# A fused attention and feed-forward kernel: 512-token steps in a fixed order, and scores on the four corners of the array

## The chip, the cores and the metric

The kernel runs on one core of a Trainium2 chip. The metric is device time in microseconds of one execution. Before the change the median of three runs is 714.71 us (709.36, 714.71, 715.33). The profile comes from one further execution, which took 712.24 us.

In the profile, PE is the matrix engine and PEld its loading of the stationary operand, DVE the vector engine, ACT the scalar (activation) engine, POOL the GpSimd engine, and SP the engine whose queue issues all DMA transfers here. Matrix products are written to accumulation memory (PSUM), which the kernel uses as eight banks of 128 rows x 512 float32.

## The reference

Attention with a narrow window and block summaries, and a feed-forward layer on its result (float32 throughout; batch 4, 8 heads, 768 tokens, head dimension 64; model width 512, hidden width 2048):

```python
block, window = 32, 16
k_sum = k.reshape(B, H, nb, block, D).max(axis=3)
v_sum = v.reshape(B, H, nb, block, D).mean(axis=3)
scores_l = scale * (q @ k^T), masked to |i - j| < window
scores_s = scale * (q @ k_sum^T) + log(block)
a = softmax(concatenate([scores_l, scores_s], -1))
attn = a @ concatenate([v, v_sum])
x = attn with heads side by side, as (3072 tokens, 512)
h = x @ w_in
out = (h * tanh(softplus(h))) @ w_out
```

The gate h * tanh(softplus(h)) is the activation that the code calls Mish. The feed-forward weights arrive as 64-bit floats and are converted on the chip.

## The kernel before

**Chunks and units.** The 3072 tokens are cut into 12 chunks of 256 (CH); three chunks make a batch element. Attention is done in units: one chunk and one pair of heads (HP = 4 pairs), so 48 units. A unit handles its 256 queries in four blocks of 64 (NQ = 4, QT = 64). Each block sees 96 keys of its window and the 24 block summaries, 120 columns (KA).

**One unit.** `att_load_keys` and `att_load_values` (L200 to L229) have SP fetch the unit's queries, window keys and window values; POOL copies the key summaries beside the window keys, a DMA copies the value summaries. For the first chunk of a batch, `key_summaries` and `value_summaries` (L163, L176) load all keys and values of the head pair into `stage` buffers, and DVE reduces them. `att_scores` (L240) does the scores. From chunk 1 on the two heads of a pair are done in one matmul per block: the host lays the queries out as a block-diagonal 128x128 operand (head 0 in rows and columns 0 to 63, head 1 in 64 to 127, zeros elsewhere), and the 128 rows of the second operand are the keys of both heads. In the first chunk the two heads are separate matmuls, each on its own 64 rows and 64 columns:

```python
nc.tensor.matmul(ps[:, s * KA:(s + 1) * KA], u["qk"][:, s, 0:P], u["qk"][:, s, P:],
                 start=True, stop=True)
```

DVE then adds the mask, scales and takes the row minimum of the negated scores (L261), ACT takes exponentials with their sum (L266), DVE the reciprocal (L269, L270), and POOL multiplies (L271). `att_transpose` (L274) turns the four blocks on PE and ACT copies them out; `att_values` (L283) multiplies with the values, each head into its own 64 columns of the array, over 120 rows. The result is split in a high part (ACT, L296) and a rest (DVE, L297), `xh` and `xl`, so that three matmuls on rounded operands replace one float32 matmul.

**Feed-forward steps.** A step is (c, fp): chunk c, and fp a pair of the 16 blocks of 128 hidden features. `ff_in` (L303) does 2 x 4 x 3 = 24 matmuls of 256 columns into one bank; `ff_act` (L317) applies Mish on ACT and splits into `gh` and `gl`; `ff_out` (L329), two steps later, does 2 x 2 x 3 = 12 matmuls of 512 columns into two output banks that stay in use over the chunk's eight steps. The first two chunks' steps are interleaved, so that each new weight block serves twice (16 steps); chunks 2 to 11 follow one after another (80 steps).

**Weights.** `load_weight` (L107) loads a 128x512 block of 64-bit floats into a `stage` buffer (3 buffers); DVE, ACT and POOL rebuild float32 from the two halves of the bits and split it (L116 to L125). 32 such blocks are done once, in the first part.

**Order.** The program is written step by step (L381 to L399): `ff_in` and `ff_act` of step i, scores or values of the units due, weight loads, `ff_out` of step i - 2, and transposes. This is only a priority: a planner with costs of its own then orders every engine's instructions, and may pull work of later steps forward where operands and buffers are free. The table `at` sets a unit's scores at some step k, its transposes at k + 1 and its values at k + 2. Chunk 2's four units have k = 7, 9, 11, 13; chunk c > 2 has its units during chunk c - 1, one every two steps. Queries, keys and values are requested one unit ahead (L391).

**Banks.** Two banks for `ff_in` (`ps_h`), four for outputs (`ps_o`), two for all attention from chunk 1 on (`ps_a`).

Of the kernel before, what the change touches and what calls it, by code (L numbers as in the profile page):

```python
# [36 lines left out]
NP_ = NFC // 2  # L37
EARLY = 10
NR = (S - CH) // P
LEAD = 4  # L40
AHEAD = 3
# [14 lines left out]
def fused_kernel(ctx: ExitStack, tc: tile.TileContext, q0, qk, kt, v0, vw, vs, w_in, w_out, out):  # L56
# [32 lines left out]
    nc.gpsimd.memset(first[:, 0:WIN], NEG / SCALE)  # L89
    last = const.tile([P, KA], F32, name="last")  # L90
    nc.gpsimd.tensor_copy(last, base)
    nc.gpsimd.memset(last[:, KW - WIN:KW], NEG / SCALE)
# [14 lines left out]
    def load_weight(src, hi, lo, name):  # L107
# [4 lines left out]
        f = ff.tile([P, WP], F32, tag="f", name=f"{name}_f", bufs=3)  # L112
        x = ff.tile([P, WP], U32, tag="x", name=f"{name}_x", bufs=2)
# [48 lines left out]

    def key_summaries(b, hp):  # L163

        if b == 0:
            ks = first_att.tile([P, WIN + S], F32, tag="ks", name=f"ks{b}_{hp}")
            nc.gpsimd.memset(ks[:, 0:WIN], 0.0)
        else:
            ks = stage.tile([P, WIN + S], F32, tag="stage", name=f"ks{b}_{hp}")
        nc.sync.dma_start(ks[:, WIN:], kt[b, hp])  # L170
        km = att.tile([P, NB], F32, tag="km", name=f"km{b}_{hp}", bufs=HP + 2)
        nc.vector.reduce_max(km, ks[:, WIN:].rearrange("p (n j) -> p n j", j=BLK), axis=AX.X)
        summary[b, hp] = [km]
        return ks

    def value_summaries(b, hp):  # L176
# [16 lines left out]
        vsum = stage.tile([VP, BLK, BLK], F32, tag="stage", name=f"vsum{b}_{hp}")  # L193
        nc.sync.dma_start(vsum, vs[b, hp].rearrange("p (d j) -> p d j", j=BLK))
# [40 lines left out]
    def att_psum(c, name):  # L235

        pool, tag = (ps_o, "o") if c == 0 else (ps_a, "a")
        return pool.tile([P, 512], F32, tag=tag, name=name)

    def att_scores(c, hp):  # L240
        u = units[c, hp]
        th = c % CPB
        ps = att_psum(c, f"sc{c}_{hp}")
        for s in range(NQ):
            if c > 0:
                nc.tensor.matmul(ps[:, s * KA:(s + 1) * KA], u["qk"][:, s, 0:P], u["qk"][:, s, P:],  # L246
                                 start=True, stop=True)
                continue
            for h in range(2):
                r = slice(h * D, (h + 1) * D)  # L250
                q = u["q"][r, s * QT:(s + 1) * QT]
                nc.tensor.matmul(ps[r, s * KA:s * KA + KW], q, u["k"][r, s * QT:s * QT + KW],
                                 start=True, stop=True)
                nc.tensor.matmul(ps[r, s * KA + KW:(s + 1) * KA], q, summary[0, hp][0][r, :],
                                 start=True, stop=True)
        pr = (att if c else first_att).tile([P, NQ, KA], F32, tag="pr", name=f"pr{c}_{hp}")

        nm = small.tile([P, NQ], F32, tag="nm", name=f"nm{c}_{hp}")
        for s in range(NQ):
            m = first if th == 0 and s == 0 else last if th == CPB - 1 and s == NQ - 1 else base  # L260
            nc.vector.tensor_tensor_reduce(  # L261
                out=pr[:, s, :], in0=ps[:, s * KA:(s + 1) * KA], in1=m, scale=-SCALE,
                scalar=-NEG, op0=ALU.add, op1=ALU.min, accum_out=nm[:, s:s + 1])
        sm = small.tile([P, NQ], F32, tag="sm", name=f"sm{c}_{hp}")
        for s in range(NQ):
            nc.scalar.activation(pr[:, s, :], pr[:, s, :], AF.Exp, scale=-1.0, bias=nm[:, s:s + 1],  # L266
                                 accum_out=sm[:, s:s + 1])
        rs = small.tile([P, NQ], F32, tag="rs", name=f"rs{c}_{hp}")
        nc.vector.tensor_scalar_add(rs, sm, 1e-9)  # L269
        nc.vector.reciprocal(rs, rs)  # L270
        nc.gpsimd.tensor_mul(pr, pr, rs.unsqueeze(2).broadcast_to([P, NQ, KA]))  # L271
        u["p"] = pr
# [10 lines left out]
    def att_values(c, hp):  # L283
        u = units.pop((c, hp))
        if c not in xs:
            xs[c] = (xp.tile([P, HP, CH], F32R, tag="xh", name=f"xh{c}"),
                     xp.tile([P, HP, CH], F32R, tag="xl", name=f"xl{c}"))
        xh, xl = xs[c]
        ps = att_psum(c, f"x_ps{c}_{hp}")
        for s in range(NQ):  # L290
            for h in range(2):
                d = slice(h * D, (h + 1) * D)
                x = ps[d, s * QT:(s + 1) * QT]
                pt = u["pt"][:, s, h * QT:(h + 1) * QT]
                nc.tensor.matmul(x, u["v"][:, s, d], pt, start=True, stop=True)  # L295
        nc.scalar.copy(xh[:, hp, :], ps[:, :CH])  # L296
        nc.vector.tensor_sub(xl[:, hp, :], ps[:, :CH], xh[:, hp, :].bitcast(F32))  # L297
# [5 lines left out]
    def ff_in(c, fp):  # L303
        i = c, fp
        xh, xl = xs[c]

        pool, tag = (ps_a, "a") if c == NCH - 1 and fp in (NP_ - 1, NP_ - 3) else (ps_h, "h")
        ph = pool.tile([P, 2, CH], F32, tag=tag, name=f"ph{c}_{fp}")
        for j in range(2):
            wh, wl = (weight(0, part, 2 * fp + j) for part in range(2))  # L310
            for cc in range(NCC):
                for n, (w, x) in enumerate(((wh, xh), (wh, xl), (wl, xh))):
                    nc.tensor.matmul(ph[:, j, :], w[:, cc * P:(cc + 1) * P], x[:, cc, :],  # L313
                                     start=(cc == 0 and n == 0), stop=(cc == NCC - 1 and n == 2))
        st[i] = {"h": ph.rearrange("p j t -> p (j t)")}

    def ff_act(c, fp):  # L317

        s = st[c, fp]
        g = ff.tile([P, 2 * CH], F32, tag="g", name=f"g{c}_{fp}", bufs=3)  # L320
        nc.scalar.activation(g, s["h"], AF.Mish)  # L321
        gh = ff.tile([P, 2 * CH], F32R, tag="gh", name=f"gh{c}_{fp}", bufs=3)
        gl = ff.tile([P, 2 * CH], F32R, tag="gl", name=f"gl{c}_{fp}", bufs=3)
# [120 lines left out]
```

## Time and profile before

| | |
|---|---|
| runs, us | 709.36, 714.71, 715.33; median 714.71 |
| profiled execution, us | 712.24 |
| its span, us | 710.5 |
| PE busy | 672.8 us (95%), 4960 matmul records |
| PEld busy | 603.6 us (85%) |
| DVE busy | 301.1 us (42%) |
| ACT busy | 354.2 us (50%) |
| POOL busy | 111.5 us (16%) |
| mean granted PE clock | 0.976 |
| DMA | 70.56 MB, mean 99 GB/s |

The span is the time from the first to the last instruction; the execution's own time has 1.7 us more around it. Busy shares are means over stages: the first quarter of the span, in which the weights are converted, looks different from the rest, so the stages have to be read apart. Matmuls are pipelined, and a matmul's own duration (291 ns for 256 columns) overlaps the next one's; what one costs in a dense row is read from the distance of the starts. A name such as `po<-w_early_out_hi,gh` says which tile is written from which; "x12" is a count. A float32 matmul appears as two records.

### The profile page before, as it was taken

To read this page: it belongs to the slowest core of one execution; us is meant where nothing else is said; L and a number is where in the kernel's file an instruction comes from. 1 tells how busy PE (TensorE), PEld (TensorE's weight loads), DVE (VectorE), ACT (ScalarE), POOL (GpSimd) and SP (SyncE) were. 2 spreads that over 40 slices of the span, in tenths; PEclk is the share of its full clock that TensorE was granted. 3 is DMA by queue.
4 is the path that set the end of the run, shared out by engine and by line. 5 is a ranking of instruction groups with operands and counts; after the bars stand their busy time and mean duration, and the time that the engine had idled before them with its cause. 6 is when DMAs were issued, how large, how long until landed. Compare 5 with 4: busy or idle time off the path is not lost.

```text
span 710.5 us, 12644 instructions
## 1 busy us (share of the span) xinstructions
PE 672.8 (95%) x4960; PEld 603.6 (85%) x4960; DVE 301.1 (42%) x872; ACT 354.2 (50%) x776; POOL 111.5 (16%) x151
## 2 busy tenths in 40 slices
PE   4978788799999999999999999999999999999998
PEld 3767677688898998998998998998998998998996
DVE  4899989952322334443223233222222322322211
ACT  2767755544556644644644644644644644644110
POOL 3454554301010010010100100100100100010000
PEclk9969899899999999999999999999999999999999
DMA  9876655772221323531311311311311311300000
GB/s 276 239 235 204 184 171 155 216 230 88 88 71 44 111 56 104 161 89 43 116 43 43 116 43 44 117 44 43 116 43 43 117 43 44 115 15 1 30 1 30
DMA packets 30683, 70.56 MB, mean 99 GB/s; under 512 B 4768, under 2 KB 9504, under 8 KB 30624
## 3 DMA queue, kind: packets, MB, share of 16 engines
q1 hardware_dynamic: 30624, 69.76, 32.2%
q8 instruction: 39, 0.64, 0.4%
q14 instruction: 20, 0.16, 0.1%
HBM read 61.15 MB, written 6.29 MB: 95 GB/s over the span
## 4 chain that ended last, share of the span: by engine, by line
PE 79%; DVE 11%; DMA 4%; issue 2%; ACT 2%; SPq 0%; POOL 0%; DVEq 0%; POOLq 0%
PE ph L313 34%; PE po L340 33%; PE sc L246 6%; PE x_ps L295 3%; DVE w_x L116 3%; PE pt_ps L278 2%; DVE w_x L117 2%; DVE w_f L122 2%; DMA ks<-kt 1%; DMA vsum<-vs 1%; DMA vw<-vw 1%; DVE w_f L120 1%; ACT pr L266 1%; DVE gl L326 1%; DVE vq L196 1%
## 5 line engine op out<-in xcount | busy, mean ns | idle before, releaser
L313 PE MATMUL ph<-xh,w_early_in_hi 128*128 128x256 f32 x480 | 138.7, 291 | 3.2 <-ACT w_early_in_hi L124 2.4
L313 PE MATMUL ph<-xh,w_early_in_lo 128*128 128x256 f32 x480 | 139.1, 291 | 2.2 <-POOL w_early_in_lo L125 2.2
L313 PE MATMUL ph<-xl,w_early_in_hi 128*128 128x256 f32 x480 | 138.9, 290 | 1.2 <-DVE xl L297 1.2
L325 DVE CAST gh<-g 128x512 fp32r<-128x512 f32 x80 | 34.3, 429 | 209.3 <-ACT g L321 196.6
L271 POOL TENSOR_TENSOR pr<-pr,rs 128x480 f32<-128x480 f32 x48 | 49.0, 1021 | 348.2 <-DVE rs L270 309.7
L313 PEld LDWEIGHTS ph<-xh,w_early_in_hi 128*128 128x128 f32 x480 | 93.9, 196 | 7.1 <-ACT w_early_in_hi L124 3.2
L313 PEld LDWEIGHTS ph<-xl,w_early_in_hi 128*128 128x128 f32 x480 | 93.8, 196 | 3.9 <-DVE xl L297 1.7
L313 PEld LDWEIGHTS ph<-xh,w_early_in_lo 128*128 128x128 f32 x480 | 93.9, 196 | 3.2 <-POOL w_early_in_lo L125 2.6
L340 PE MATMUL po<-w_early_out_hi,gh 128*128 128x512 f32 x240 | 94.3, 396 | 2.5 <-ACT gh L325 2.5
L340 PE MATMUL po<-w_early_out_hi,gl 128*128 128x512 f32 x240 | 95.6, 398 | 0.0
L340 PE MATMUL po<-w_early_out_lo,gh 128*128 128x512 f32 x240 | 95.0, 396 | 0.0
L321 ACT ACTIVATE g<-ph 128x512 f32<-128x512 f32 x96 | 57.4, 598 | 67.0 <-PE ph L313 66.5
L313 PE MATMUL ph<-xh,w_late_in_hi 128*128 128x256 f32 x288 | 82.5, 287 | 0.1
L313 PE MATMUL ph<-xh,w_late_in_lo 128*128 128x256 f32 x288 | 81.9, 284 | 0.1
L313 PE MATMUL ph<-xl,w_late_in_hi 128*128 128x256 f32 x288 | 81.1, 282 | 0.0
L266 ACT ACTIVATE pr<-pr,nm 128x120 f32<-128x120 f32 x192 | 73.7, 385 | 5.8 <-DVE nm L261 5.3
L321 ACT ACT_TABLE_LOAD x44 | 56.5, 1283 | 38.7 <-PE ph L313 38.3
L326 DVE TENSOR_TENSOR gl<-g,gh 128x512 fp32r<-128x512 f32 x96 | 70.7, 736 | 8.1 <-ACT gh L325 5.5
L296 ACT CAST xh<-x_ps 128x256 fp32r<-128x256 f32 x48 | 17.9, 372 | 100.7 <-PE x_ps L295 100.7
L280 ACT COPY pt<-pt_ps 120x512 f32<-120x512 f32 x48 | 28.1, 586 | 71.9 <-PE pt_ps L278 71.5
L266 ACT ACT_TABLE_LOAD x43 | 55.2, 1283 | 8.4 <-DVE nm L261 7.8
L340 PE MATMUL po<-w_late_out_hi,gl 128*128 128x512 f32 x144 | 56.7, 394 | 1.6 <-DVE gl L326 1.6
(75 smaller groups left out, 1149.9 us busy)
## 6 DMA issues: line engine op xcount, KB each, us to landing
qk<-qk SPq DMA_DIRECT2D x44, 496.0 KB
vw<-vw SPq DMA_DIRECT2D x48, 192.0 KB
w<-w_in SPq DMA_DIRECT2D x16, 512.0 KB
w<-w_out SPq DMA_DIRECT2D x16, 512.0 KB
ks<-kt SPq DMA_DIRECT2D x16, 384.0 KB
out<-o SPq DMA_DIRECT2D x24, 256.0 KB
vsum<-vs SPq DMA_DIRECT2D x12, 384.0 KB
vw<-vm SPq DMA_DIRECT2D x44, 48.0 KB
```

The costliest lines, as they stand in the source:

```text
L116: nc.vector.tensor_scalar(out=x, in0=low, scalar1=29, scalar2=None, op0=ALU.logical_shift_right)
L246: nc.tensor.matmul(ps[:, s * KA:(s + 1) * KA], u["qk"][:, s, 0:P], u["qk"][:, s, P:], start=True, stop=True)
L266: nc.scalar.activation(pr[:, s, :], pr[:, s, :], AF.Exp, scale=-1.0, bias=nm[:, s:s + 1], accum_out=sm[:, s:s + 1])
L271: nc.gpsimd.tensor_mul(pr, pr, rs.unsqueeze(2).broadcast_to([P, NQ, KA]))
L280: nc.scalar.copy(pt.rearrange("p s q -> p (s q)"), ps[:KA, :])
L295: nc.tensor.matmul(x, u["v"][:, s, d], pt, start=True, stop=True)
L296: nc.scalar.copy(xh[:, hp, :], ps[:, :CH])
L313: nc.tensor.matmul(ph[:, j, :], w[:, cc * P:(cc + 1) * P], x[:, cc, :], start=(cc == 0 and n == 0), stop=(cc == NCC - 1 and n == 2))
L321: nc.scalar.activation(g, s["h"], AF.Mish)
L325: (nc.scalar.copy if c < 2 else nc.vector.tensor_copy)(gh, g)
L326: nc.vector.tensor_sub(gl, g, gh.bitcast(F32))
L340: nc.tensor.matmul(po[c][t], g[:, tok], w, start=(fc == 0 and n == 0), stop=(fc == NFC - 1 and n == 2))
```

## The change

- **Steps.** From the second pair of chunks on, a step is (g, fc): a pair of chunks (TG = 512 tokens) and one block of 128 hidden features. `ff_in` then has 4 x 3 = 12 matmuls of 512 columns, and `ff_out` 4 x 3 = 12 of 512 into four output banks, one for each 128 tokens. There are again 80 such steps. The first pair keeps its 256-token steps. `xh` and `xl` hold a pair of chunks.
- **Order.** The 80 steps are inside `tc.manual_schedule()`: each engine does its instructions in the order of the program. The first 16 steps are still ordered by the planner. Chunk 2's units have k = 6, 7, 8, 9 and chunk 3's k = 10, 11, 12, 13; later units come one every two steps during the pair of chunks before theirs. In an iteration: `ff_in`, Mish, values (of the unit two steps before), scores, split, normalization, loads, `ff_out` of step i - 2, transposes (of the unit one step before).
- **Scores.** Each block and head is a matmul of its own, on 64 rows (the head) and 64 columns (odd or even block), so that a block pair of both heads uses the four 64x64 corners. The zeros of the block-diagonal layout are no longer read, though still loaded. Each head writes into a bank of its own, so a unit's scores take two banks.
- **Banks and buffers.** `ff_in`, scores, transposes and values share four banks (`ps_w`); four remain for outputs. The weight scratch, the activations and the output copies share six buffers (before: 3 + 2, 3 and 2).
- **Smaller.** Summaries are requested two units ahead (`load_ahead`); the output copies alternate between ACT and DVE; the edge masks hold only for the half of the rows with the first or last block.

The diff, cut:

```diff
+LEAD = 4
+CG = 2
+TG = CG * CH
+NG = NCH // CG
...
-    xp = ctx.enter_context(tc.tile_pool(name="xp", bufs=3))
+    xp = ctx.enter_context(tc.tile_pool(name="xp", bufs=2))
...
-    ff = ctx.enter_context(tc.tile_pool(name="ff", bufs=2))
-    ps_h = ctx.enter_context(tc.tile_pool(name="ps_h", bufs=2, space=PS))
+    ff = ctx.enter_context(tc.tile_pool(name="ff", bufs=6))
     ps_o = ctx.enter_context(tc.tile_pool(name="ps_o", bufs=4, space=PS))
-    ps_a = ctx.enter_context(tc.tile_pool(name="ps_a", bufs=2, space=PS))
+
+    ps_w = ctx.enter_context(tc.tile_pool(name="ps_w", bufs=4, space=PS))
...
-        f = ff.tile([P, WP], F32, tag="f", name=f"{name}_f", bufs=3)
-        x = ff.tile([P, WP], U32, tag="x", name=f"{name}_x", bufs=2)
+        f = ff.tile([P, WP], F32, tag="t", name=f"{name}_f")
+        x = ff.tile([P, WP], F32, tag="t", name=f"{name}_x").bitcast(U32)
...
+    def load_summaries(b, hp):
+
+        ks = stage.tile([P, S], F32, tag="stage", name=f"ks{b}_{hp}")
+        nc.sync.dma_start(ks, kt[b, hp])
+        vsum = stage.tile([VP, BLK, BLK], F32, tag="stage", name=f"vsum{b}_{hp}")
+        nc.sync.dma_start(vsum, vs[b, hp].rearrange("p (d j) -> p d j", j=BLK))
+        sources[b, hp] = ks, vsum
...
+            keys = ks = sources[b, hp][0]
...
+        vsum = sources.pop((b, hp))[1]
...
-        ps = att_psum(c, f"sc{c}_{hp}")
+        ps = [att_psum(c, f"sc{c}_{hp}_{h}") for h in range(2)]
         for s in range(NQ):
-            if c > 0:
-                nc.tensor.matmul(ps[:, s * KA:(s + 1) * KA], u["qk"][:, s, 0:P], u["qk"][:, s, P:],
-                                 start=True, stop=True)
-                continue
             for h in range(2):
                 r = slice(h * D, (h + 1) * D)
+                row, at0 = slice(s % 2 * QT, (s % 2 + 1) * QT), s // 2 * KA
+                if c > 0:
+                    nc.tensor.matmul(ps[h][row, at0:at0 + KA], u["qk"][r, s, h * QT:(h + 1) * QT],
+                                     u["qk"][r, s, P:], start=True, stop=True)
+                    continue
...
-        for s in range(NQ):
-            m = first if th == 0 and s == 0 else last if th == CPB - 1 and s == NQ - 1 else base
+        for j in range(NQ):
+            h, pair = divmod(j, NQ // 2)
+            m = first if th == 0 and pair == 0 else last if th == CPB - 1 and pair == NQ // 2 - 1 else base
             nc.vector.tensor_tensor_reduce(
-                out=pr[:, s, :], in0=ps[:, s * KA:(s + 1) * KA], in1=m, scale=-SCALE,
-                scalar=-NEG, op0=ALU.add, op1=ALU.min, accum_out=nm[:, s:s + 1])
+                out=pr[:, j, :], in0=ps[h][:, pair * KA:(pair + 1) * KA], in1=m, scale=-SCALE,
+                scalar=-NEG, op0=ALU.add, op1=ALU.min, accum_out=nm[:, j:j + 1])
...
+    def att_normalize(c, hp):
+        u = units[c, hp]
+        pr = u["p"]
         rs = small.tile([P, NQ], F32, tag="rs", name=f"rs{c}_{hp}")
-        nc.vector.tensor_scalar_add(rs, sm, 1e-9)
+        nc.vector.tensor_scalar_add(rs, u["sm"], 1e-9)
         nc.vector.reciprocal(rs, rs)
         nc.gpsimd.tensor_mul(pr, pr, rs.unsqueeze(2).broadcast_to([P, NQ, KA]))
...
+        g, half = divmod(c, CG)
+        if g not in xs:
+            xs[g] = (xp.tile([P, HP, TG], F32R, tag="xh", name=f"xh{g}"),
+                     xp.tile([P, HP, TG], F32R, tag="xl", name=f"xl{g}"))
+        xh, xl = (x[:, hp, half * CH:(half + 1) * CH] for x in xs[g])
...
-                pt = u["pt"][:, s, h * QT:(h + 1) * QT]
+                pt = u["pt"][:, h * NQ // 2 + s // 2, s % 2 * QT:(s % 2 + 1) * QT]
...
-    def ff_in(c, fp):
-        i = c, fp
-        xh, xl = xs[c]
-
-        pool, tag = (ps_a, "a") if c == NCH - 1 and fp in (NP_ - 1, NP_ - 3) else (ps_h, "h")
-        ph = pool.tile([P, 2, CH], F32, tag=tag, name=f"ph{c}_{fp}")
-        for j in range(2):
-            wh, wl = (weight(0, part, 2 * fp + j) for part in range(2))
+    def parts(step):
+
+        if len(step) == 2:
+            return [step[1]], step[0], 0, TG
+        _, c, fp = step
+        return [2 * fp, 2 * fp + 1], 0, c * CH, CH
+
+    def ff_in(step):
+        fcs, g, at0, n = parts(step)
+        xh, xl = (x[:, :, at0:at0 + n] for x in xs[g])
+        ph = ps_w.tile([P, len(fcs), n], F32, tag="w", name=f"ph{step[0]}_{step[-1]}_{at0}")
+        for j, fc in enumerate(fcs):
+            wh, wl = (weight(0, part, fc) for part in range(2))
             for cc in range(NCC):
-                for n, (w, x) in enumerate(((wh, xh), (wh, xl), (wl, xh))):
+                for k, (w, x) in enumerate(((wh, xh), (wh, xl), (wl, xh))):
                     nc.tensor.matmul(ph[:, j, :], w[:, cc * P:(cc + 1) * P], x[:, cc, :],
-                                     start=(cc == 0 and n == 0), stop=(cc == NCC - 1 and n == 2))
-        st[i] = {"h": ph.rearrange("p j t -> p (j t)")}
+    def ff_act(step):
+
+        name = f"{step[0]}_{step[1]}_{step[-1]}"
+        a = ff.tile([P, TG], F32, tag="t", name=f"a{name}")
+        nc.scalar.activation(a, st[step], AF.Mish)
+        st[step] = a, *(ff.tile([P, TG], F32R, tag=f"a{part}", name=f"a{part}{name}", bufs=3) for part in "hl")
+
+    def ff_split(step):
+
+        a, ah, al = st[step]
+
+        (nc.scalar.copy if len(step) == 3 else nc.vector.tensor_copy)(ah, a)
+        nc.vector.tensor_sub(al, a, ah.bitcast(F32))
...
+    def ff_out(step):
+        _, ah, al = st.pop(step)
+        fcs, g, at0, n = parts(step)
+        for t in range(n // P):
+            row = g * TG + at0 + t * P
+            if fcs[0] == 0:
+                po[row] = ps_o.tile([P, DM], F32, tag="o", name=f"po{row}")
+            for j, fc in enumerate(fcs):
+                tok = slice(j * n + t * P, j * n + (t + 1) * P)
-                for n, (g, w) in enumerate(((gh, wh), (gl, wh), (gh, wl))):
-                    nc.tensor.matmul(po[c][t], g[:, tok], w,
-                                     start=(fc == 0 and n == 0), stop=(fc == NFC - 1 and n == 2))
-        if fp == NP_ - 1:
-            for t in range(CH // P):
-                o = ff.tile([P, DM], F32, tag="o", name=f"o{c}_{t}")
-                nc.scalar.copy(o, po[c][t])
-                nc.sync.dma_start(out[c * CH + t * P:c * CH + (t + 1) * P, :], o)
+                for k, (a, w) in enumerate(((ah, wh), (al, wh), (ah, wl))):
+                    nc.tensor.matmul(po[row], a[:, tok], w,
+                                     start=(fc == 0 and k == 0), stop=(fc == NFC - 1 and k == 2))
+            if fcs[-1] == NFC - 1:
+                o = ff.tile([P, DM], F32, tag="t", name=f"o{row}")
+                (nc.vector.tensor_copy if t % 2 else nc.scalar.copy)(o, po.pop(row))
+                nc.sync.dma_start(out[row:row + P, :], o)
...
+    steps = [(0, c, i - c * LEAD) for i in range(NP_ + LEAD) for c in range(CG) if 0 <= i - c * LEAD < NP_]
+    first_steps = len(steps)
+    steps += [(g, fc) for g in range(1, NG) for fc in range(NFC)]
...
+    for c, hp in todo[HP:]:
+        g, half = divmod(c, CG)
+        u = half * HP + hp
+        k = max(hp - 1, 0) if c == 1 else first_steps - 2 * HP - 2 + u if g == 1 else (g - 2) * NFC + first_steps + 2 * u - 1
+        at.setdefault(k, []).append((c, hp))
...
+    def load_ahead(c, hp):
+
+        unit = todo[min(todo.index((c, hp)) + 2, len(todo) - 1)]
+        if unit[0] % CPB == 0:
+            load_summaries(unit[0] // CPB, unit[1])
...
+    for i in range(first_steps):
+        ff_in(steps[i])
+        ff_act(steps[i])
+        ff_split(steps[i])
+        for unit in at.get(i - 2, ()):
+            att_values(*unit)
+        for unit in at.get(i, ()):
+            att_scores(*unit)
+            att_normalize(*unit)
+            load_next(keys, att_load_keys)
+            load_next(values, att_load_values)
+            load_ahead(*unit)
...
+    with tc.manual_schedule():
+        for i in range(first_steps, len(steps) + 2):
+            if i < len(steps):
+                ff_in(steps[i])
+                ff_act(steps[i])
+            for unit in at.get(i - 2, ()):
+                att_values(*unit)
+            for unit in at.get(i, ()):
+                att_scores(*unit)
+            if i < len(steps):
+                ff_split(steps[i])
+            for unit in at.get(i, ()):
+                att_normalize(*unit)
+                load_next(keys, att_load_keys)
+                load_ahead(*unit)
+            for _ in at.get(i - 2, ()):
+                load_next(values, att_load_values)
+            ff_out(steps[i - 2])
+            for unit in at.get(i - 1, ()):
+                att_transpose(*unit)
```

More of the change, by code (lines that the diff above doesn't have):

```diff
@@ L88, in fused_kernel @@
     nc.gpsimd.tensor_copy(first, base)
-    nc.gpsimd.memset(first[:, 0:WIN], NEG / SCALE)
+    nc.gpsimd.memset(first[0:QT, 0:WIN], NEG / SCALE)
     last = const.tile([P, KA], F32, name="last")
     nc.gpsimd.tensor_copy(last, base)
-    nc.gpsimd.memset(last[:, KW - WIN:KW], NEG / SCALE)
+    nc.gpsimd.memset(last[QT:P, KW - WIN:KW], NEG / SCALE)
     def weight_tiles(pool, name, blocks):
@@ new lines, in ff_in @@
+        st[step] = ph.rearrange("p j t -> p (j t)")
+    def ff_act(step):
[7 more added lines that the diff above has]
+        nc.vector.tensor_sub(al, a, ah.bitcast(F32))
@@ L349, in fused_kernel @@
     todo = [(c, hp) for c in range(NCH) for hp in range(HP)]
-    steps = [(c, i - c * LEAD) for i in range(NP_ + LEAD) for c in range(2) if 0 <= i - c * LEAD < NP_]
-    steps += [(c, fp) for c in range(2, NCH) for fp in range(NP_)]
+    steps = [(0, c, i - c * LEAD) for i in range(NP_ + LEAD) for c in range(CG) if 0 <= i - c * LEAD < NP_]
+    first_steps = len(steps)
+    steps += [(g, fc) for g in range(1, NG) for fc in range(NFC)]
     begins = {"K": lambda n: att_load_keys(0, n), "V": lambda n: att_load_values(0, n),
-              "S": lambda n: att_scores(0, n), "T": lambda n: att_transpose(0, n),
+              "S": lambda n: (att_scores(0, n), att_normalize(0, n)), "T": lambda n: att_transpose(0, n),
@@ L365, in fused_kernel @@
     at = {}
-    start = 0
-    for c in range(1, NCH):
-        n = steps.index((c, 0)) - start
-        for hp in range(HP):
-            k = min(start + n - 3, start + n - 3 - 2 * (HP - 1 - hp) if c == 2 else start + n * hp // HP - 1)
-            at.setdefault(max(k, 0), []).append((att_scores, c, hp))
-            at.setdefault(max(k, 0) + 1, []).append((att_transpose, c, hp))
-            at.setdefault(max(k, 0) + 2, []).append((att_values, c, hp))
-        start += n
-    def turn(k, lag):
-        return k + lag - (k >= len(steps) - AHEAD)
@@ L380, in fused_kernel @@
-    loaded = HP + 1
-    for i in range(len(steps) + 2):
-        parts = at.get(i, ())
-        now = [x for k, x in enumerate(steps) if turn(k, 0) == i]
-        for x in now:
-            ff_in(*x)
-        for x in now:
-            ff_act(*x)
-        for f, c, hp in parts:
-            if f is not att_transpose:
-                f(c, hp)
-                if f is att_scores and loaded < len(todo):
-                    att_load(*todo[loaded])
-                    loaded += 1
+    for c, hp in todo[HP:]:
[3 more added lines that the diff above has]
+        at.setdefault(k, []).append((c, hp))
@@ new lines, in fused_kernel, with load_next @@
+    keys = iter(todo[HP + 1:])
+    values = iter(todo[HP + 1:])
+    def load_ahead(c, hp):
+        unit = todo[min(todo.index((c, hp)) + 2, len(todo) - 1)]
+        if unit[0] % CPB == 0:
+            load_summaries(unit[0] // CPB, unit[1])
+    def load_next(units, load):
+        if unit := next(units, None):
+            load(*unit)
+    for i in range(first_steps):
[10 more added lines that the diff above has]
+            load_ahead(*unit)
@@ L394, in fused_kernel @@
         load_weights(4 if i < LEAD else 2)
         if i >= 2:
-            ff_out(*steps[i - 2])
-        for f, c, hp in parts:
-            if f is att_transpose:
-                f(c, hp)
+            ff_out(steps[i - 2])
[18 more added lines that the diff above has]
+                load_next(values, att_load_values)
+            ff_out(steps[i - 2])
+            for unit in at.get(i - 1, ()):
+                att_transpose(*unit)
```

47 lines of the change are left out of this document (12 added, 35 removed).

## The prediction, made before the run

> **What bounds the kernel now.** I read the stretches first (busy time of each engine in a stretch), then the chain of work that ended last, then the timeline of single instructions. The columns of a stretch are its length, then busy us (instructions) of PE, PEld, DVE, ACT and POOL, the granted clock, the DMA share and GB/s.
>
> ```profile
> 100.00:120.00 20.00, 18.18 (x122) 15.62 (x122) 20.00 (x29) 10.25 (x18) 8.43 (x7) 0.99 0.54 159
> ```
>
> ```profile
> 180.00:710.50 530.50, 527.04 (x3902) 476.81 (x3900) 160.26 (x571) 249.76 (x539) 44.50 (x70) 1.00 0.22 66
> ```
>
> The kernel has two stages. In the first, DVE is full (20.00 of 20.00 us). In the second, three quarters of the span, PE is busy 527.04 of 530.50 us at clock 1.00 and DVE and ACT for under half of it. So an edit counts in the second stage only by what it does to PE's own stream, and in the first by DVE. The chain in order of time (start, length, what) splits that stream:
>
> ```profile
> 391.83 1.82 PE po L340 x8
> ...
> 401.53 0.61 PE x_ps L295 x16
> 402.14 1.08 PE sc L246 x8
> 403.23 0.94 PE po L340 x4
> 404.17 2.86 PE ph L313 x24
> 407.03 2.75 PE po L340 x12
> 409.78 1.32 PE ph L313 x11
> 411.10 0.44 PE pt_ps L278 x4
> ...
> 445.20 1.82 PE po L340 x8
> ```
>
> One step is 2.86 us of first-layer matmuls and 2.75 us of second-layer ones. One attention unit (a chunk and a pair of heads) is 0.61 values + 1.08 scores + 0.44 transposes = 2.13 us, the changes between kinds of matmul included. A chunk has 8 steps and 4 units: 8 x 5.61 + 4 x 2.13 = 53.40 us; the same place of the pattern comes again after 445.20 - 391.83 = 53.37. Nothing is missing, so there is no stall to remove here: only cheaper PE work helps.
>
> **The 512-token steps.** From the second pair of chunks on, a step has 12 first-layer matmuls of 512 columns in place of 24 of 256. The second layer already issues 128x512 matmuls of the same type: 2.75 / 12 = 0.229 us each, against 2.86 / 24 = 0.119 for 256 columns. Twelve at that price are 2.75: 0.11 us less per step, and 80 steps give -8.8 us. The second layer keeps its 12 per step.
>
> The Trainium skill (TensorE: Matmul & The Clock Gate, "Back-to-back issue gap") gives N/2.4 + 2.5 ns for the gap at full clock; as an estimate from that page a step would win 24 x 109.2 - 12 x 215.8 = 31 ns, and 80 steps 2.5 us. The rows above do not agree: per matmul they show 0.119 and 0.229, a fixed part of about 9 ns, and it is by them that the sum goes.
>
> **The scores.** PE's timeline of one unit (start, length, line, out<-in, count):
>
> ```profile
> 401.46 0.69 PE L295 MATMUL x_ps<-pt,vw 120*64 120x64 f32 x16
> 402.07 1.15 PE L246 MATMUL sc<-qk 128*128 128x120 f32 x8
> 402.99 0.48 PE L340 MATMUL po<-w_late_out_lo,gh 128*128 128x512 f32 x1
> ```
>
> The four score matmuls show as 8 records in 402.99 - 402.07 = 0.92 us, 0.115 each. The change makes them 16 records on 64x64 corners, each with the same 120 columns. All depends on how many run at once. At the start of the kernel the first chunk's scores use two corners, opposite ones:
>
> ```profile
> 23.15 0.24 PE L254 MATMUL sc<-km,q 64*64 64x24 f32 x2
> 23.32 0.69 PE L295 MATMUL x_ps<-pt,vw 120*64 120x64 f32 x16
> ```
>
> ```profile
> 27.63 0.39 PE L252 MATMUL sc<-ks,q 64*64 64x96 f32 x4
> 27.84 0.26 PE L254 MATMUL sc<-km,q 64*64 64x24 f32 x4
> 27.93 0.38 PE L252 MATMUL sc<-ks,q 64*64 64x96 f32 x4
> ```
>
> Eight records take 27.93 - 27.63 = 0.30 us, 38 ns each; at 0.115 us per 120 columns they would need 4 x 92 + 4 x 23 = 460 ns one after another, so opposite corners overlap. The values, two column halves on all rows, also take 38 ns a record (0.61 / 16). No row shows two row halves over the same columns. The ends are therefore: four at once, 4 x 0.115 = 0.46 us a unit (-0.46); two at once, 8 x 0.115 = 0.92 (nothing won); none, 16 x 0.115 = 1.84 (+0.92). I take 16 x 0.038 = 0.61 us, -0.31, because both rows nearest to it, opposite corners and column halves, come to 38 ns whatever the column count. The change from values to corners is new; from 23.15, two records at 38 ns would let x_ps start at 23.23 and it starts at 23.32, so a change of form costs up to 0.10 us. I charge it whole. A unit falls to 2.13 - 0.31 + 0.10 = 1.92.
>
> By the Trainium skill (TensorEngine Tiling, "Key Properties") a change of tiling mode drains the array, which speaks against going to corners for so short a burst; the 0.10 us is what this trace shows of it.
>
> Units 12 to 47 (chunks 3 to 11), 36 of them, run where PE is the bound: 36 x -0.21 = -7.6 us. Those before lie beside DVE's work and win nothing.
>
> **The first stage.** DVE's groups of 30 to 134 us (count, busy us, mean ns):
>
> ```profile
> L116 DVE TENSOR_SCALAR w_x<-w 128x512 uint32<-128x512 uint32 x28 | 26.9, 964 | 0.0
> L122 DVE SCALAR_TENSOR_TENSOR w_f<-w_f,w_x 128x512 uint32<-128x512 uint32 x29 | 23.0, 794 | 0.0
> L117 DVE SCALAR_TENSOR_TENSOR w_x<-w,w_x 128x512 uint32<-128x512 uint32 x28 | 22.6, 811 | 0.0
> L120 DVE TENSOR_SCALAR w_f<-w_f 128x512 f32<-128x512 f32 x29 | 15.2, 524 | 2.6 <-ACT w_f L119 2.6
> ```
>
> The weights take 87.7 of these 104 us, and that work is not changed. What moves: units of chunk 2 go from steps 7, 9, 11, 13 to 6 to 9, and chunk 3's, once in the second stage, to steps 10 to 13. So two units of chunk 2 pass ahead of the last weights. Before, the third of them comes after the weights:
>
> ```profile
> 146.55 1.15 PE L246 MATMUL sc<-qk 128*128 128x120 f32 x8
> ```
>
> ```profile
> L261 DVE CUSTOM_DVE_ANT_0 pr<-sc,base 128x120 f32<-128x120 f32 x160 | 36.3, 277 | 8.4 <-PE sc L246 8.1 <-issue 0.4
> ```
>
> ```profile
> L297 DVE TENSOR_TENSOR xl<-x_ps,xh 128x256 fp32r<-128x256 f32 x48 | 20.2, 421 | 82.8 <-ACT xh L296 82.7
> ```
>
> Such a unit puts 4 x 0.277 + 0.421 = 1.5 us on DVE, and about 0.4 more by estimate for the sums' reciprocals: two units, +3.8 us for the weights. PE has 2 x 2.13 = 4.3 us less to do afterwards. Net nothing. Chunk 3's units run behind the weights either way, on PE, so moving them is neutral. Their queues are not: each brings its score, value and summary loads on SP and one copy and one multiplication on POOL, and SP takes the first summaries (3 staging buffers, shared with the weights) ahead of the last four weights. What that can do stands in the trace:
>
> ```profile
> 129.17 5.47 DMA ks<-kt
> ```
>
> ```profile
> 139.33 1.11 PE L278 MATMUL pt_ps<-ident,pr 128*120 128x128 f32 x4 [4.17 <-POOL pr L271]
> 140.09 0.78 PE L340 MATMUL po<-w_early_out_hi,gl 128*128 128x512 f32 x1
> 140.66 0.63 PE L340 MATMUL po<-w_early_out_lo,gh 128*128 128x512 f32 x1
> 141.09 0.63 PE L340 MATMUL po<-w_early_out_hi,gh 128*128 128x512 f32 x1
> ```
>
> DVE reached a summary whose keys had not landed; the softmax behind it was late, PE stood 4.17 us and then issued 512 columns every 0.43 us instead of 0.23 for some ten matmuls: about 6 us in all. The change asks for the summaries one unit earlier, which removes this (-6), and packs four such units one per step, which can repeat it. I take 0 and keep -6 and +25 (four times) as ends. Six buffers for what had ten (weight scratch, activations, output copies) belong to the same risk.
>
> **The fixed order.** In a pair of steps PE now does first layer, values, scores, second layer, first layer, second layer, transposes. Each consumer needs cover:
>
> ```profile
> 406.22 0.18 DVE L270 RECIPROCAL rs<-rs 128x4 f32<-128x4 f32 x1
> ```
>
> ```profile
> L271 POOL TENSOR_TENSOR pr<-pr,rs 128x480 f32<-128x480 f32 x48 | 49.0, 1021 | 348.2 <-DVE rs L270 309.7
> ```
>
> ```profile
> L321 ACT ACTIVATE g<-ph 128x512 f32<-128x512 f32 x96 | 57.4, 598 | 67.0 <-PE ph L313 66.5
> ```
>
> ```profile
> L321 ACT ACT_TABLE_LOAD x44 | 56.5, 1283 | 38.7 <-PE ph L313 38.3
> ```
>
> ```profile
> L345 ACT COPY o<-po 128x512 f32<-128x512 f32 x24 | 13.7, 578 | 17.0 <-PE po L340 17.0
> ```
>
> From the scores' start (402.07) to the reciprocal's end it is 4.3 us, with POOL's multiplication 5.4; the transposes come 0.8 + 3 x 2.75 = 9.0 us after it: 3.6 us to spare. An activation with its table load frees its bank 1.9 us after the first layer's end, and the next first layer starts at least 2.75 us later. At the end of a group all four output banks are in use; two copies each on ACT and DVE behind the softmax end about 4.3 + 2 x 0.58 = 5.5 us after the scores' start, and the bank is wanted after the rest of that second layer and one first layer, 0.8 + 2 x 2.75 = 6.3 us. All covered, the last by under 1 us; uncovered it costs at most a few us over five group ends. Loads are issued one unit, 12 us, ahead. I price the order at nothing.
>
> **Sum**, against the profiled execution's own 712.24 us (span 710.5): -8.8 - 7.6 + 0 = -16.4, so 695.8; I say 696. That execution lies 2.5 us under the median of the runs shown (714.71), inside their 6 us spread.
>
> **The rivals.**
>
> More is won: four corners at once (-16.6 with no charge for the change of form) and the 6 us stall gone: 712.24 - 8.8 - 16.6 - 6 = 681. For it: the row halves feed separate banks. Against: every overlapped row shows 38 ns a record, and 16 of them are 0.61.
>
> The corners don't do what they say: row halves over the same columns wait for each other, scores cost 0.92 as before plus the 0.10: 712.24 - 8.8 + 3.6 = 707. For it: the trace has no such pair. If not even the opposite corners overlapped, 36 x 1.02 gives 740; the 0.30 us speak against that.
>
> Slower: batch 1's summaries hold DVE in order, and each of the four units at steps 10 to 13 repeats the stall and the half clock of 139 us: 696 + 25 = 721. It needs all four; three give 715, within 1%. For it: DVE is full there and 5.47 us were waited for one landing. Against: loads two units ahead.
>
> **Chances.** Forecast 0.52, more won 0.20, corners without gain 0.13, first-stage stalls 0.12, no overlap 0.03. The range 681 to 712 reaches from the better case over the forecast (by itself 688 to 703) to the corners without gain, and leaves out the last two cases and a little beneath. About 1% (7 us) is what a measurement of this kernel can tell: faster than 707.6 us have the first two cases and more than half of the third, 0.79; within 1% 0.09; slower 0.12.
>
> **What would show it.** Right: first layer in twelve records at 0.229 us spacing; the score visit near 0.77 us in place of 1.08, 16 records; a group of 16 steps and 8 units taking 16 x 5.50 + 8 x 1.92 = 103.4 us against 2 x 53.37 = 106.7; no PE wait above 1 us past the first pair. Wrong: score records at 0.058 us or more; waits of the first layer for the scores' or the copies' banks; transposes waiting for POOL between 120 and 180 us with a clock under 1.00; 512 columns slower with the activations moving than with the weights moving.

## The result, and the profile after

The changed kernel takes 693.85 us (median of four runs, 692.95 to 694.62) against 712.79 for the kernel before beside it: a ratio of 0.9737, 95% interval 0.9687 to 0.9787. A second set of runs gave 694.55 us, 0.9762 (0.9736 to 0.9788). The forecast was 696. The profiled execution took 693.84 us, its span is 692.1: 18.4 us less than before.

The stretch from 180 us on (length; busy us of PE, PEld, DVE, ACT, POOL; clock; DMA share; GB/s) is as dense as it was:

```profile
180.00:692.10 512.10, 507.39 (x3134) 408.40 (x3133) 162.32 (x549) 220.03 (x479) 37.80 (x62) 1.00 0.22 69
```

The chain of work that ended last, one unit and two steps:

```profile
398.04 0.62 PE x_ps L319 x16
398.65 0.57 PE sc L264 x16
399.22 2.99 PE po L371 x12
402.21 2.76 PE ph L342 x12
404.97 2.75 PE po L371 x12
407.72 0.44 PE pt_ps L301 x4
408.15 2.76 PE ph L342 x12
410.91 0.62 PE x_ps L319 x16
```

Twelve first-layer matmuls take 2.76 us where 24 took 2.86. Sixteen score records take 0.57 us where eight took 1.08 with the change of kind behind them; that change now shows as a longer second layer behind the scores (2.99 for 2.75). A pair of steps with one unit is 410.91 - 398.04 = 12.87 us; before it was 53.37 / 4 = 13.34.

Rows of the kernel before and of the changed one cut both spans into three: up to the first matmul of the first later step, up to PE's last matmul, and the rest. Before, in PE's timeline and in the chain's end:

```profile
174.92 0.28 PE L313 MATMUL ph<-xh,w_early_in_hi 128*128 128x256 f32 x1
```

```profile
707.06 0.02 issue
707.08 0.58 ACT o L345
```

After, the same two views, and PE's waits (total us, times, longest) between 40 and 150 us:

```profile
183.80 0.50 PE L342 MATMUL ph<-xh,w_early_in_hi 128*128 128x512 f32 x1
```

```profile
687.41 0.02 issue
687.43 0.69 DVE o L375
```

```profile
PE po L371 <- ACT ah L357: 13.2, 6, 5.1
PE po L371 <- DVE al L358: 4.9, 3, 2.7
```

The first stage is 183.80 - 174.92 = 8.9 us longer, the second 503.6 instead of 532.1, so 28.5 shorter, the tail 4.7 instead of 3.4, 1.3 longer: 18.4 in all, before rounding. In the second stage, 80 steps by 0.10 are 8 us. The 36 units are 0.31 cheaper each: 11.2. Chunk 3's four units and the scores of the next one now lie before the cut: 4 x 1.82 + 0.77 = 8.1. So do the transposes and values of chunk 2's last unit, 0.44 + 0.61 = 1.0 us, which before came behind it:

```profile
175.99 0.60 PE L278 MATMUL pt_ps<-ident,pr 128*120 128x128 f32 x4
180.58 0.69 PE L295 MATMUL x_ps<-pt,vw 120*64 120x64 f32 x16
```

Together 28.3. So the first stage took over 9.1 us of PE work and is 8.9 longer. PE's last wait, 1.9 us, ends at 149.7 us.

### The profile page after: what moved, and what is told of

Read it like the earlier page. It is cut to its first block, busy times and chain, and to the rows that moved or that the text cites. A ratio compares the mean times of both kernels' runs of the same rounds, so it can differ in the third digit from the quotient of the medians.

```text
span 692.1 us, 11422 instructions
## 1 busy us (share of the span) xinstructions
PE 651.8 (94%) x4352; PEld 525.5 (76%) x4352; DVE 301.4 (44%) x884; ACT 347.7 (50%) x764; POOL 113.6 (16%) x151
## 4 chain that ended last, share of the span: by engine, by line
PE 81%; DVE 9%; ACT 3%; DMA 3%; issue 1%; SPq 0%; POOL 0%; DVEq 0%; ACTq 0%
PE po L371 36%; PE ph L342 35%; PE x_ps L319 4%; PE sc L264 3%; PE pt_ps L301 3%; DVE w_x L119 2%; DVE w_x L120 2%; DVE w_f L123 2%; DVE w_f L125 1%; DMA w<-w_out 1%; PE vm_ps L202 1%; DMA vw<-vw 1%; ACT pr L284 1%; ACT L350 1%; DMA vsum<-vs 1%
## 5 line engine op out<-in xcount | busy, mean ns | idle before, releaser
L371 PE MATMUL po<-w_early_out_hi,ah 128*128 128x512 f32 x240 | 98.9, 418 | 12.6 <-ACT ah L357 12.4
L342 PE MATMUL ph<-xh,w_early_in_hi 128*128 128x512 f32 (+1 forms) x280 | 103.9, 371 | 1.6 <-ACT xh L320 1.6
L371 PE MATMUL po<-w_early_out_hi,al 128*128 128x512 f32 x240 | 98.4, 410 | 4.9 <-DVE al L358 4.9
L342 PE MATMUL ph<-xl,w_early_in_hi 128*128 128x512 f32 (+1 forms) x280 | 101.3, 362 | 0.4 <-DVE xl L321 0.2
L342 PE MATMUL ph<-xh,w_early_in_lo 128*128 128x512 f32 (+1 forms) x280 | 101.2, 361 | 0.0
L371 PE MATMUL po<-w_early_out_lo,ah 128*128 128x512 f32 x240 | 96.8, 403 | 0.0
L358 DVE TENSOR_TENSOR al<-a,ah 128x512 fp32r<-128x512 f32 x96 | 66.5, 692 | 12.6 <-ACT ah L357 9.6
L350 ACT ACT_TABLE_LOAD x44 | 56.5, 1283 | 28.5 <-issue 14.8
L342 PE MATMUL ph<-xh,w_late_in_hi 128*128 128x512 f32 (+1 forms) x168 | 61.8, 368 | 0.0
L342 PEld LDWEIGHTS ph<-xh,w_early_in_hi 128*128 128x128 f32 x280 | 53.1, 190 | 10.7 <-ACT xh L320 2.1
L342 PE MATMUL ph<-xh,w_late_in_lo 128*128 128x512 f32 (+1 forms) x168 | 60.6, 361 | 0.0
L342 PE MATMUL ph<-xl,w_late_in_hi 128*128 128x512 f32 (+1 forms) x168 | 60.4, 359 | 0.0
L371 PEld LDWEIGHTS po<-w_early_out_hi,al 128*128 128x128 f32 x240 | 47.1, 196 | 16.4 <-DVE al L358 7.4
```

Of the source, the lines that this page charges most:

```text
L350: nc.scalar.activation(a, st[step], AF.Mish)
L358: nc.vector.tensor_sub(al, a, ah.bitcast(F32))
L371: nc.tensor.matmul(po[row], a[:, tok], w, start=(fc == 0 and k == 0), stop=(fc == NFC - 1 and k == 2))
```

## The experiments

Each is the changed kernel with one edit. All times are medians, beside the kernel before on the same chip.

### Scores over the whole array again

```diff
+            if c > 0:
+                nc.tensor.matmul(ps[0][:, s * KA:(s + 1) * KA], u["qk"][:, s, 0:P], u["qk"][:, s, P:],
+                                 start=True, stop=True)
+                continue
```

(with the masks, the order of `pr` and the values' index of the kernel before)

> The changed kernel with the scores of chunks 1 to 11 again as one matmul per block over the whole array (block-diagonal queries, one bank), all else as changed. In the changed kernel a score visit is 0.57 us + 0.20 for the change to the next kind; before it was 1.08. My theory (records of overlapping corners cost 36 to 38 ns, whole-array ones 115) expects 1.08 again, 0.31 more for each of the 36 units that run where PE is the bound: +11 us on 693.8, so 705. The sum on record, with 0.10 us charged for the change of form, would give +7.6: 701.5. The rival that the corners win nothing expects 694.

706.48 us, ratio 0.9922 (0.9880 to 0.9964). Its chain:

```profile
403.92 0.62 PE x_ps L329 x16
404.54 1.08 PE sc L267 x8
405.62 2.74 PE po L381 x12
```

The score visit is 1.08 us again, against 0.57 + 0.24 here (2.99 for 2.75), and the second stage 513.5 us for 503.6, with 31 score visits in it: 9.9 / 31 = 0.32 each. The corners give what the records' spacing says, and the 0.10 us charged for the change from values to corners is not there. The profiled execution is 10.3 us above the changed kernel's, 9.9 of them in this stage; the medians are 12.6 apart.

### First layer in halves of 256 columns

```diff
+            for at in range(0, n, CH):
...
-                    nc.tensor.matmul(ph[:, j, :], w[:, cc * P:(cc + 1) * P], x[:, cc, :],
+                        nc.tensor.matmul(ph[:, j, at:at + CH], w[:, cc * P:(cc + 1) * P], x[:, cc, at:at + CH],
```

> The changed kernel with each 512-column first-layer matmul of the 80 later steps done as two of 256 columns (24 per step, each half accumulated by itself), all else as changed. My theory (a fixed 9 ns per matmul) expects 24 x 0.119 = 2.86 us for 2.75, +0.11 us a step, +8.8 us: 702.6. A fixed 2.5 ns per matmul, the figure of the Trainium skill (TensorE: Matmul & The Clock Gate, Back-to-back issue gap), would give 31 ns a step, +2.5 us: 696.3. If the gain came from the order and the banks alone, 694.

703.36 us, ratio 0.9866 (0.9815 to 0.9918).

```profile
403.52 2.87 PE ph L343 x24
406.39 2.75 PE po L372 x12
```

The step has its 2.87 us back. The second stage is 511.2 us, 7.6 more than 503.6: near the 8.8 expected, 7.9 ns for each of the 80 x 12 further matmuls. The Trainium skill (TensorE: Matmul & The Clock Gate, "Back-to-back issue gap") has 2.5 ns of fixed cost in its formula for an isolated matmul; by that it would be an estimated 2.4 us, and the measurement differs. The same section says that in a stream of weight loads and matmuls, as here, both set the spacing.

### Row halves over the same columns

```diff
-        for s in range(NQ):
+        for s in (0, 2, 1, 3):
```

> The changed kernel with the blocks of a unit's scores in the order 0, 2, 1, 3: now eight records in a row use the two row halves over the same columns, then eight over the other columns, and opposite corners never alternate. If row halves over the same columns overlap like the others (the open point of the prediction), the score visit stays at 0.57 us and the time at 694. If they wait for each other, all 16 records run one after another, 16 x 0.115 = 1.84 us: +1.27 us for 36 units, 739. If half of the overlap is lost, 0.92 us: 706.

698.74 us (two runs), ratio 0.9800 (0.9755 to 0.9845). PE's chain:

```profile
404.43 0.58 PE sc L264 x16
405.01 2.98 PE po L371 x12
```

0.58 us: two row halves over the same columns, each writing into a bank of its own, overlap like any other pair, which the trace of before could not show. The profiled execution, 699.88 us, is 6.0 above the changed kernel's; only 0.7 of that is in the second stage (504.3 us), and the first later step began at 189.22 us, 5.4 later.

### All steps in the planner's order

```diff
-    with tc.manual_schedule():
+    if True:
```

> The changed kernel with the 80 later steps ordered by the planner again instead of in the order of the program, all else as changed. My theory (the fixed order is worth nothing by itself, since PE had no stall in the second stage before either) expects 694 within 3 us, PE dense from the end of the weights on. The rival that the fixed order is part of the gain expects PE waits in the second stage, for banks or for the softmax, and over 700.

698.65 us, ratio 0.9811 (0.9768 to 0.9854), and once more with more rounds:

> The same kernel as the one with all steps in the planner's order, with more rounds, since its interval of 0.977 to 0.985 touched that of the changed kernel (0.974 to 0.979). Theory after the first look: the fixed order gains nothing in the second stage, but keeps the second batch's summaries out of the first stage, where the planner pulls them forward into DVE's queue; expected ratio 0.980 to 0.983, 3 to 5 us behind the fixed order. The rival, that the fixed order is worth nothing at all: 0.975 to 0.978.

699.57 us, 0.9793 (0.9767 to 0.9819). Both lie behind the fixed order (0.9737, 0.9762), but the intervals touch: a gain of 3 to 5 us from the fixed order is likely, not settled. A place for it can be read. PE's timeline and the key loads for summaries on SP, planner's order (the first row of each list is the last of one batch):

```profile
195.46 0.40 PE L342 MATMUL ph<-xh,w_early_in_hi 128*128 128x512 f32 x1
```

```profile
149.40 0.34 SPq L171 DMA_DIRECT2D ks<-kt  x1
153.81 0.34 SPq L171 DMA_DIRECT2D ks<-kt  x1
157.61 0.36 SPq L171 DMA_DIRECT2D ks<-kt  x1
164.04 0.34 SPq L171 DMA_DIRECT2D ks<-kt  x1
168.50 0.35 SPq L171 DMA_DIRECT2D ks<-kt  x1
```

and in the fixed order:

```profile
143.76 0.34 SPq L171 DMA_DIRECT2D ks<-kt  x1
246.55 0.67 SPq L171 DMA_DIRECT2D ks<-kt  x1
```

The second stage is 503.3 us from that row, equal to the fixed order's 503.6, so the order gains nothing there. The planner pulls the next batch's summaries into the end of the first stage, the fixed order leaves them at 246 us. That they are what costs the time was not tested. The profiled execution, 705.36 us, is the longest of its set, so its 195.46 overstates the difference.

### Summaries one unit ahead

```diff
-        unit = todo[min(todo.index((c, hp)) + 2, len(todo) - 1)]
+        unit = todo[min(todo.index((c, hp)) + 1, len(todo) - 1)]
```

(with `load_ahead` before `load_next`)

> The changed kernel with the keys and values for the block summaries requested one unit ahead instead of two, as before the change; all else as changed. The step on record said that two units ahead takes away the wait of DVE for the keys, and with it about 6 us of PE stall and half clock: 700 here, with a PE wait of some 4 us for transposes in the first stage. The rival: the planner and the three staging buffers decide when these loads go out, so nothing changes: 694.

695.03 us, ratio 0.9759 (0.9727 to 0.9792), beside the changed kernel itself in the same set:

> The changed kernel as it is, beside the three that follow on the same chip, and as a second profile of the same program: 694 within 4 us. The second stage (from the first 512-token step to the last matmul) should again be 503.5 us; if executions differ, they should differ by the first stage alone.

694.55 us, 0.9762. The medians show no difference, so the earlier request is not worth the 6 us that the prediction gave it. But the profiled execution with one unit ahead, 699.57 us, is the longest of its four, and in it transposes wait for POOL again after 30 us, which they do in neither profile of the changed kernel:

```profile
PE pt_ps L301 <- POOL pr L295: 3.1, 2, 2.4
```

Such waits also stand in profiles of runs below that request two units ahead: 2.3 us with less DVE work, 2.1 with the activations' copy on POOL, 2.9 with both edits at the end. So the request alone does not decide about them, and what took the stalls of before away stays open. The second profile of the changed kernel has a second stage of 503.6 us again, from 183.81 to 687.42.

### Less DVE work on the weights

```diff
-        nc.vector.tensor_scalar(out=x, in0=low, scalar1=29, scalar2=None, op0=ALU.logical_shift_right)
-        nc.vector.scalar_tensor_tensor(out=x, in0=high, scalar=SIGN, in1=x,
-                                       op0=ALU.bitwise_and, op1=ALU.bitwise_or)
+        nc.vector.tensor_scalar(out=x, in0=high, scalar1=SIGN, scalar2=None, op0=ALU.bitwise_and)
```

> The changed kernel with DVE's two operations on the low halves of the weights' bits (0.84 + 0.88 us in the first stage) replaced by one on the sign alone, so the weights lose their last bits; all else as changed. My theory that DVE bounds the first stage expects 32 x about 0.9 = 28 us less DVE work, of which the first 512-token step comes earlier by 15 to 25 us (PE's own work is the next limit): 670 to 680. If transfers or ACT bound that stage, 690 to 694.

684.03 us, ratio 0.9615 (0.9586 to 0.9645): 10 us, not 15 to 25. PE's longest waits up to 190 us were still for the activations' copy:

```profile
PE po L369 <- ACT ah L355: 14.8, 4, 5.4
```

DVE is spared less than expected: its operations on the weights between 30 and 147 us take 63.6 us instead of 86.1, 22.5 less, not 28, because those that are left get longer, the last from 824 to 1010 ns. And it now waits for ACT:

```profile
L123 DVE SCALAR_TENSOR_TENSOR w_f<-w_f,w_x 128x512 uint32<-128x512 uint32 x28 | 28.3, 1010 | 0.3
L121 DVE TENSOR_SCALAR w_f<-w_f 128x512 f32<-128x512 f32 x28 | 17.2, 615 | 9.0 <-ACT w_f L120 8.8
```

DVE is a bound of the first stage, but not the only one: somewhat under half of what it is spared reaches PE, whose first later step comes 9.8 us earlier.

### Weights earlier

```diff
-        load_weights(4 if i < LEAD else 2)
+        load_weights(4)
```

> The changed kernel with four weight blocks asked for in every step until all are loaded, instead of four in the first four steps and two after, so that the last weights stand ahead of chunk 2's and 3's units in the planner's priority; all else as changed. If the units that passed ahead of the weights cost PE (it waited 18 us in the first stage for activations behind DVE's and ACT's queues), the weights end 5 to 10 us earlier and the time is 688 to 691. If what PE gains there it loses later to the units' softmax, 694.

695.38 us, ratio 0.9776 (0.9746 to 0.9807): nothing gained. The last weight operation on DVE, in the changed kernel and in this one:

```profile
145.22 1.79 DVE L125 SCALAR_TENSOR_TENSOR w_f<-w_f,w_x 128x512 uint32<-128x512 uint32 x1
```

```profile
135.48 0.68 DVE L125 SCALAR_TENSOR_TENSOR w_f<-w_f,w_x 128x512 uint32<-128x512 uint32 x1
```

The weights end 11 us earlier and the kernel does not: the first later step begins at 186.90 us, 3.1 later than in the changed kernel. That PE lost to the units behind the weights what it gained there would fit, but is not shown.

### The activations' copy on POOL

```diff
-        (nc.scalar.copy if len(step) == 3 else nc.vector.tensor_copy)(ah, a)
+        (nc.gpsimd.tensor_copy if len(step) == 3 else nc.vector.tensor_copy)(ah, a)
```

> The changed kernel with the rounding copy of the activations in the first 16 steps on POOL instead of ACT; all else as changed. PE waited 12 to 13 us in the first stage for that copy. If ACT's queue is what it waited for, the first 512-token step comes 3 to 8 us earlier: 687 to 691. If the wait is the whole chain from matmul over activation and copy to the difference, which PE's order left uncovered, a slower copy on POOL makes it longer: 695 to 700.

692.87 us (three runs; a fourth took 702.44), ratio 0.9702 (0.9676 to 0.9729, from the three). In PE's waits the 13.2 us for the copy became

```profile
PE po L371 <- DVE al L358: 9.9, 5, 3.4
PE po L371 <- POOL ah L357: 7.1, 6, 2.8
```

together 17 for 18: the wait is the chain from the matmul to the split, whoever copies. The ratio hints at a few us won; its interval overlaps that of the changed kernel's first set and lies just under that of the second (0.9736 to 0.9788), so it is not settled.

### The weights' last operation on DVE

```diff
-        nc.gpsimd.tensor_sub(lo, f, hi.bitcast(F32))
+        nc.vector.tensor_sub(lo, f, hi.bitcast(F32))
```

> The changed kernel with the last operation of each weight block (block minus its rounded part) on DVE instead of POOL; all else as changed. In the trace DVE operations of 0.41 us take 1.5 us where they start beside such a POOL operation, as if they waited for its end. If that is so, DVE gets 28 operations of 0.68 us more and loses about 28 waits of 1.1 us, some 12 us in all, and the first stage shortens by about a third of that (28 us less DVE work gave 10): 689 to 692. If DVE's long operations have another cause, 19 us more work on DVE: 698 to 702.

684.68 us, ratio 0.9605 (0.9568 to 0.9642): the lowest of all, 10 us below the changed kernel, and more than expected. What was suspected is in the timeline of the changed kernel, POOL above DVE:

```profile
106.69 1.77 POOL L128 TENSOR_TENSOR w_late_out_lo<-w_f,w_late_out_hi 128x512 fp32r<-128x512 f32 x1 [3.42 <-ACT w_late_out_hi L127]
107.23 1.52 DVE L119 TENSOR_SCALAR w_x<-w 128x512 uint32<-128x512 uint32 x1
```

POOL is done at 108.46, DVE's operation at 108.75: 0.29 us later, where it takes 0.41 alone. The operation with two inputs at 145.22 us, shown above, is another: POOL's ran from 145.17 to 146.46, and DVE's ended 0.55 us after it and took 1.79 us for 0.68. DVE's groups from 30 to 147 us in the changed kernel, and with this edit:

```profile
L123 DVE TENSOR_SCALAR w_f<-w_f 128x512 f32<-128x512 f32 x28 | 17.1, 617 | 0.8 <-ACT w_f L122 0.8
```

```profile
L119 DVE TENSOR_SCALAR w_x<-w 128x512 uint32<-128x512 uint32 x28 | 22.3, 821 | 1.3 <-DMA w<-w_out 1.2
```

```profile
L123 DVE TENSOR_SCALAR w_f<-w_f 128x512 f32<-128x512 f32 x28 | 12.2, 434 | 1.9 <-ACT w_f L122 1.7
L119 DVE TENSOR_SCALAR w_x<-w 128x512 uint32<-128x512 uint32 x28 | 11.7, 445 | 0.9 <-DMA w<-w_in 0.4 <-DMA w<-w_out 0.3
```

821 becomes 445 ns and 617 becomes 434. The first later step begins at 173.14 us, 10.7 earlier, and the second stage is 503.5.

The Trainium skill (GPSIMD Engine Reference, "Specifications") says that POOL's memory interfaces are shared with DVE, with contention for some DVE forms; this trace agrees, with 1.52 us for 0.41.

The waits of DVE are thus shown, but not that they are the whole gain. The 30 to 147 us as a stretch (after the length, the third figure in us is DVE's busy time, the fifth POOL's), in the changed kernel and with this edit:

```profile
30.00:147.00 117.00, 94.24 (x701) 75.61 (x699) 104.20 (x220) 82.13 (x173) 54.29 (x43) 0.88 0.58 186
```

```profile
30.00:147.00 117.00, 98.29 (x779) 80.22 (x778) 104.15 (x262) 83.39 (x187) 14.71 (x19) 0.91 0.60 202
```

DVE is as busy as before (104.15 for 104.20 us): its four weight operations take 65.2 us for 86.1, and the 28 moved ones add 19.4. What became shorter is the chain of a weight block, whose last operation takes 0.69 us on DVE for 1.48 on POOL, and POOL is free. Which of these the 10 us come from, or whether a new order of the stage by the planner has a part in it, was not separated.

### Both

> The changed kernel with both edits of the last two runs: the weight blocks' last operation on DVE and, in the first 16 steps, the rounding copy of the activations on POOL. If the two gains add (3 us and 10 us), the ratio is 0.956 to 0.958, about 681. If the copies on POOL hold DVE up as the weights' POOL operations did, 16 copies cost some of it again: 0.960 to 0.964, 684 to 687.

689.55 us, ratio 0.9672 (0.9644 to 0.9700): the gains do not add, and the copies on POOL lose 5 us of the 10. The reason expected for that is there only in small part: L119 takes 442 ns, as without them, and a few DVE operations that begin beside such a copy take 0.3 to 0.4 us longer. PE's waits for the copy and the split are 6.8 and 6.4 us, and 4.0 us of waits for ACT's copy of the transposes are new. That the planner orders the stage anew with each edit would explain it, but was not tested.

## Why the prediction was right

**Steps, -8.8.** Right, a little too much. The rows give 2.76 for 2.86 us, and putting the halves back cost 7.6 us.

**Scores, -7.6.** The mechanism was right, the size not: 36 units save 0.31 us each, 11.2 in all. The term that was off is the 0.10 us charged for the change from values to corners. It was read from a single place of the start and charged as if it came on top; in the dense stage, values end and scores begin without it. A delay of that size stands behind whole-array scores too (0.08 to 0.09 us in the trace of before), where no corners are used. The 16 records take 36 ns each, against 38 assumed. The rival of corners without gain falls by the whole-array run (9.9 us of the second stage) and by the same-column run. With the 5 score visits that moved ahead (5 x 0.32 = 1.6) the two runs that put the old forms back account for 9.9 + 1.6 + 7.6 = 19.1 of the 19.4 us that the second stage won beside the work moved out of it. The shared banks and buffers were not tested alone; little is left for them there.

**First stage, 0.** Right in sum (8.9 us for 9.1 of work moved in), wrong in its parts, and so by luck. I priced two units ahead of the last weights at 3.8 us of DVE. They passed ahead, with summaries of the next units, and the last weights came at 147.0 us, 12.7 later than before (134.3). The stretch of before, against the one of the changed kernel shown with the run that moved the weights' last operation:

```profile
30.00:134.30 104.30, 88.39 (x603) 77.25 (x599) 100.25 (x202) 70.76 (x156) 49.41 (x41) 0.89 0.62 189
```

DVE's work grew by 4.0 us (100.25 to 104.20), much as priced. The rest is DVE standing idle, 12.8 us for 4.1: I had taken it as full. The stall at 139 us I had read wrongly too, as 5.47 us waited for keys. That is the time of the transfer; DVE itself stood 0.39 us for it:

```profile
134.67 0.95 DVE L172 TENSOR_REDUCE km<-ks 128x24 f32<-128x768 f32 x1 [0.39 <-DMA ks<-kt]
135.53 1.25 DVE L269 TENSOR_SCALAR rs<-sm 128x4 f32<-128x4 f32 x1
```

The softmax's small operations stood behind the summaries in DVE's order, and the first of them took 1.25 us for 0.16, beside a POOL operation from 135.50 to 136.76. In the changed kernel this stall and the one at 160 us are gone, 7.0 us, but PE's waits for the activations' copy and split grew from 4.1 to 18.1 us; from 30 us on its waits sum to 22.6 us before and 24.2 after. The earlier request is not worth the 6 us I gave it, and why the first stage came out even stays open. The slow rival (four repeated stalls, 721) did not come.

**Fixed order, 0.** Right for the second stage: 503.3 and 503.6 us with and without it. Behind the weights it probably does save something, by what it keeps out of the first stage; I did not see that.

**Tail.** Not priced: +1.3 us. Four output transfers and a DVE copy of 0.69 us end it, for two and an ACT copy of 0.58. In the other profiles the same tail took 3.6 to 5.0 us, so how much of the 1.3 belongs to the change is not shown.

The sum, -16.4 against -18.4, is close because the misses were small and in part cancelled: 3.6 us too little for the scores, up to 0.8 too much for the steps, 1.3 of tail left out.

## What to carry to other kernels

Cut the span where the bound changes and measure each stage between two named instructions: here the second stage was 503.3 to 503.6 us in ten different executions with the same steps, while the first ran from 173 to 195 us. Where one engine is dense, price an edit by the spacing of starts in rows of the same kind, and check a one-off gap elsewhere in the trace before charging it 36 times. A stage with several engines in a chain gives back only part of what one of them is spared (22.5 us less on DVE gave 10).

## What the runs showed of the hardware

- All four 64x64 corners work side by side, same-column row halves too, with a bank for each row half: 16 float32 records of 120 columns in 0.57 us, 36 ns each, where whole-array ones take 115. The matmuls behind them come 0.10 to 0.12 us later than in a dense row; behind whole-array scores it was 0.08 to 0.09.
- A matmul of these rounded operands costs 0.119 us for 256 columns and 0.229 for 512: about 9 ns per matmul beside its columns, 7.9 by the run with halves.
- A POOL operation holds DVE's operations on the weights until it ends: a held one ends 0.28 to 0.29 us after it with one input (0.41 us became up to 1.52) and 0.55 us after it with two (0.68 became up to 1.79). DVE's reductions for the summaries (0.94 and 1.2 us) and the softmax's operations on the scores (0.27) are not held. Doing the POOL operation on DVE, at 0.69 us each, took 10 us off the kernel, with DVE as busy as before.
